# A decode block on one core: part of the wq load over eight engines, the last K tiles in between V tiles, and two products 512 columns wide with a fold

## The chip, the cores and the metric

The kernel runs on one core of a Trainium2 chip. The metric is the device time of one execution in microseconds. The kernel before takes 1319.78 us, the median of three runs (1319.77 to 1319.85).

## The reference

One token per sequence, batch 2, goes through a layer norm; then attention over a cache of 32768 positions with 8 KV heads (4 query heads each) and a gated MLP are computed from the same normed row, and their product is added to the input. All data are float32.

```python
xn = layernorm(x)                                        # [2, 1, 512]
q = (xn @ wq)                                            # 512 x 4096: 32 heads of 128
p = softmax(q @ k_cache.T * 128 ** -0.5)                 # caches: [2, 8, 32768, 128]
s = (p @ v_cache) @ wo                                   # wo: 4096 x 512
gate, up = xn @ W_gate, xn @ W_up                        # 512 x 1792 each
g = silu((gate * (gate > 0) * up) @ W_down)              # W_down: 1792 x 512
return x + s * g
```

## The kernel before

The caches are 64 tiles of 8.4 MB: each of the 16 pairs of batch and KV head (a "group", `g`) has two K tiles and two V tiles (`u` = 0, 1), and a tile holds 16384 positions as 128 partitions of 64 KB. With wq (8.4 MB), the two MLP input weights in one slot (`gu`), W_down (`wd`) and wo (8.4 MB) they all pass through one ring of three slots of 64 KB per partition (`slot`, `SLOTS`). A load is issued on SyncE's queue (`load`) and waits there until the tile three places earlier in the ring has been read for the last time. SyncE's queue is in order, so a load that waits holds back all loads behind it.

For a group, `scores(g)` lets VectorE turn each K tile in 32x32 blocks, in place, in eight parts of 128x2048 (`turn`), lets TensorE multiply the turned halves with the query (`score`, 16 matmuls a half) and lets VectorE take maxima (`peak`). `soft(g)` finds the maximum of the group, takes exponents on ScalarE, brings the weights into V's order with a matmul by a permutation (`perm`) and a transpose on VectorE, and sums them. `values(t)` is 32 matmuls of 512 columns on a V tile, into four column groups of the PSUM tile `o_ps`. `finish_group(g)` scales and masks the result into `os`; after every second group four matmuls with `place` add it to `ot_ps`. A float32 matmul stands twice in the profile: `x64` there is 32 matmuls of the source.

The loop over groups runs under a manual schedule: on each engine, instructions stand in the order in which the code is written. A group loads K, K, V, V. At the end wo comes in six pieces of 16, 8, 4, 2, 1 and 1 rows of 512 columns (a row is one `i`; partition p holds rows of its own), `ot` is taken out of `ot_ps`, and 32 rows times four column blocks of 128 are multiplied into `py` (128 small matmuls, `L418`). Two VectorE operations with `gy` (the MLP's result, computed at the start by `mlp_down`) and `xy` (the input) give the output, which leaves in four small DMAs.

The start: wq's load is the first, `gu` and `wd` follow into the other two slots, and the first K tile takes wq's slot when `project_q` has read it.

Of the kernel before, what the change touches and what calls it, by code (L numbers as in the profile page):

```python
# [20 lines left out]
SLOTS = 3  # L21
ALIGN = 512
WO_PIECES = (16, 8, 4, 2, 1, 1)


@with_exitstack
def kernel(
# [39 lines left out]
    def load(dst, src):  # L67
        nc.sync.dma_start(dst, src)

    wqs = slot("wq")  # L70
    load(wqs, wq.rearrange("(p i) n -> p (i n)", p=P))
    wqt = wqs.rearrange("p (i n) -> p i n", i=NKC)

    row = work.tile([P, 512], F32, tag="row", name="xp", bufs=3)
    xp = row[:32, :]
# [83 lines left out]
    xnp = const.tile([P, NKC, 32], F32, name="xnp")  # L159
# [3 lines left out]
    nc.vector.tensor_copy(xnp.rearrange("p k m -> p (k m)"), m_ps[:, : NKC * 32])  # L163

    def project_q():
        pick = ident.rearrange("p (c m) -> p c m", c=4)[:, :, :B]
        nq = 2 * REP * 4 * B
        spread = work.tile([P, 4, 4, Q], F32, tag="row", name="spread", bufs=3)
        for kb in range(4):
            nc.vector.tensor_copy(  # L170
                spread[:, :, kb, :], ident.rearrange("p (e l) -> p e l", e=4)
            )
        for half in range(2):
            pq = S[0][half]
            for i in range(NKC):
                for c in range(4):
                    n0 = (half * 4 + c) * 512
                    nc.tensor.matmul(  # L178
                        pq[32 * c : 32 * c + 32, :],
                        xnp[:, i, :],  # L180
                        wqt[:, i, n0 : n0 + 512],
                        start=(i == 0),
                        stop=(i == NKC - 1),
                    )
        for half in range(2):
            qs = work.tile([P, 512], F32, tag="row", name=f"qs_{half}", bufs=3)
            nc.vector.tensor_copy(qs, S[0][half])  # L187
# [56 lines left out]

    def mlp_down(ht):
        for i in range(FI):
            for c in range(4):
                nc.tensor.matmul(
                    m_ps[32 * c : 32 * c + 32, :P],
                    ht[:, i, :],  # L250
                    wdt[:, i, c * P : (c + 1) * P],
                    start=(i == 0),
                    stop=(i == FI - 1),
                )
        nc.scalar.activation(gy, m_ps[:, :P], AF.Silu)

    def group(g):
        return g % B, g // B

    def load_tile(src, t, name):  # L260
        b, hk = group(t // NU)
        lo = (t % NU) * TK
        dst = slot(name)
        load(dst, src[b, hk, lo : lo + TK, :].rearrange("(p r) d -> p (r d)", p=P))
        return dst

    MX, LS, W, RL, OS = {}, {}, {}, {}, {}

    def turn(t, s):
        k = KT[t]  # L270
        for c in range(NC):
            part = slice((s * NC + c) * NJ * DH, (s * NC + c + 1) * NJ * DH)
            nc.vector.transpose(k[:, part], k[:, part])  # L273

    def score(t, s):
        g, u = divmod(t, NU)
# [18 lines left out]
    def scores(g):  # L295
        halves = [(g * NU + u, s) for u in range(NU) for s in range(NS)]
        turn(*halves[0])
        for before, after in zip(halves, halves[1:] + [None]):
            if after:
                turn(*after)  # L300
            score(*before)
            peak(*before)

    def soft(g):
# [20 lines left out]
        for u in range(NU):  # L325
            for s in range(NS):
# [3 lines left out]
                    w, S[u][s], AF.Exp, bias=nb, scale=SCALE, accum_out=LS[g][:, i : i + 1]  # L330
                )
                nc.tensor.matmul(pt_ps, perm[:, s, :], w, start=(s == 0), stop=(s == NS - 1))  # L332
            pt = work.tile([P, NJ, Q], F32, tag="pt", name=f"pt_{g}_{u}")
            nc.vector.transpose(pt.rearrange("p j m -> p (j m)"), pt_ps)  # L334
            PT[g * NU + u] = pt
# [51 lines left out]
    mlp_down(ht)  # L387

    with tc.manual_schedule(engines=None):
        for g in range(NG):  # L390
            for u in range(NU):
                KT[g * NU + u] = load_tile(kc, g * NU + u, f"k_{g}_{u}")
            for u in range(NU):
                VT[g * NU + u] = load_tile(vc, g * NU + u, f"v_{g}_{u}")
            scores(g)
            soft(g)
            if g % 3 == 2 and g // 3 < 4:
                c = g // 3
                nc.scalar.dma_start(xy[32 * c : 32 * c + B, :], x[:, 0, c * P : (c + 1) * P])
            for u in range(NU):  # L400
                values(g * NU + u)
            finish_group(g)

        wos = slot("wo")
        worows = wo.rearrange("(p i) d -> p (i d)", p=P)
# [4 lines left out]
        for b in range(B):  # L410
            nc.vector.tensor_reduce(
                ot[:, :, b], ot_ps[:, b].rearrange("p c i -> p i c"), axis=AX.X, op=ALU.add
            )
        py = S[0][0]
        wot = wos.rearrange("p (i d) -> p i d", i=WI)
        for i in range(WI):
            for c in range(4):
                nc.tensor.matmul(  # L418
                    py[32 * c : 32 * c + B, :P],
                    ot[:, i, :],  # L420
                    wot[:, i, c * P : (c + 1) * P],
                    start=(i == 0),
                    stop=(i == WI - 1),
                )
        nc.vector.tensor_mul(res, py[:, :P], gy)
        nc.vector.tensor_add(res, res, xy)
        for c in range(4):
# [35 lines left out]
```

## Time and profile before

| | |
|---|---|
| median of three runs | 1319.78 us |
| the profiled execution's own time | 1318.75 us |
| its span, first to last instruction | 1316.9 us |
| TensorE busy | 838.3 us (64%) |
| VectorE busy | 674.7 us (51%) |
| ScalarE busy | 49.8 us (4%) |
| read from memory | 564.67 MB, 429 GB/s over the span |
| granted TensorE clock, mean | 0.854 |

An engine's busy share says little here, since the stages have different limits. What is to be looked at is the share of the sixteen DMA engines' time, and then the last 30 us, where loads run out and the output still has to be computed. In the profile, PE is TensorE (PEld its weight loads), DVE VectorE, ACT ScalarE, POOL GpSimd, SP SyncE. A row of a timeline is the start, the length, engine, line, operation and how many, and in brackets the idle time before it and what ended that. In a table of stretches, each engine's busy time stands with its number of instructions, then the granted clock of TensorE, the mean busy share of the DMA engines and GB/s.

### The profile page before, as it was taken

The numbers are of one execution on the slowest core, as the hardware profiler recorded it, in microseconds if no ns is written. First come the engines' busy times: TensorE is split into PE (matmuls) and PEld (weight loads), VectorE is DVE, ScalarE is ACT, GpSimd is POOL, SyncE is SP. The second block draws the span as 40 slices with busy tenths as digits, with TensorE's granted clock in tenths as the row PEclk, the third lists the DMA queues.
The fourth block names the chain that finished last, engine by engine and source line by source line (L and its number), as shares of the span: only waits on it lengthen the run. The fifth ranks groups of instructions, "written<-read, shape, count | busy, mean of one in ns | idle before, by whom it ended". The sixth has DMA issues, their size and how long they took to land.

```text
span 1316.9 us, 10829 instructions
## 1 busy us (share of the span) xinstructions
PE 838.3 (64%) x4892; PEld 214.5 (16%) x4892; DVE 674.7 (51%) x569; ACT 49.8 (4%) x133; POOL 0.7 (0%) x6
## 2 busy tenths in 40 slices
PE   3467466765756577575667756665675767667467
PEld 1212011110211112021121201111121111212013
DVE  3183562917447191744719265380936638183560
ACT  0000000000000000000000000000000000000000
POOL 0000000000000000000000000000000000000000
PEclk9779698988888789787888969798888878988789
DMA  9999999999999999999999999999999999999996
GB/s 407 436 442 421 442 438 426 432 438 433 430 430 440 437 424 439 434 428 442 423 435 444 423 436 442 426 432 438 427 438 428 436 435 428 444 424 433 444 422 290
DMA packets 10738, 565.36 MB, mean 429 GB/s; under 512 B 1202, under 2 KB 1218, under 8 KB 1604
## 3 DMA queue, kind: packets, MB, share of 16 engines
q1 hardware_dynamic: 10664, 564.66, 99.1%
q8 instruction: 38, 0.62, 0.2%
q14 instruction: 8, 0.07, 0.0%
q10 hardware_dynamic: 28, 0.01, 0.0%
HBM read 564.67 MB, written 0.00 MB: 429 GB/s over the span
## 4 chain that ended last, share of the span: by engine, by line
DMA 48%; DVE 27%; PE 23%; issue 2%; ACT 0%; SPq 0%; ACTq 0%; DVEq 0%
DMA k<-in_A_k_cache_dram 45%; DVE k L273 22%; PE o_ps L351 9%; PE pt_ps L332 7%; PE s L280 5%; DMA gu<-in_B_W_up_dram 3%; DVE mx L293 2%; DVE pt L334 2%; PE s L418 1%; DVE mrow L316 0%; PE m_ps L319 0%; PE m_ps L338 0%; PE m_ps L307 0%; ACT w L329 0%; DVE mr L309 0%
## 5 line engine op out<-in xcount | busy, mean ns | idle before, releaser
L280 PE MATMUL s<-k,qt 128*32 128x512 f32 x2048 | 465.0, 687 | 362.8 <-DVE k L273 362.6
L273 DVE STREAM_TRANSPOSE k<-k 128x2048 f32<-128x2048 f32 x256 | 566.8, 2276 | 193.0 <-DMA k<-in_A_k_cache_dram 187.3
L351 PE MATMUL o_ps<-v,pt 128*16 128x512 f32 x2048 | 223.4, 592 | 0.2
L280 PEld LDWEIGHTS s<-k,qt 128*32 128x32 f32 x2048 | 87.9, 121 | 735.8 <-DVE k L273 593.1
L363 DVE SCALAR_TENSOR_TENSOR os<-o_ps,rl,mask 128x512 f32<-128x512 f32 x16 | 12.0, 750 | 220.3 <-PE o_ps L351 220.3
L332 PE MATMUL pt_ps<-w,perm 128*128 128x512 f32 x128 | 86.0, 808 | 32.3 <-ACT w L329 17.9
L329 ACT ACTIVATE w<-s,nb 128x512 f32<-128x512 f32 x64 | 43.3, 685 | 1178.4 <-DVE nb L323 1176.4
L351 PEld LDWEIGHTS o_ps<-v,pt 128*16 128x16 f32 x2048 | 57.9, 97 | 151.3 <-issue 146.7
L334 DVE STREAM_TRANSPOSE pt<-pt_ps 128x512 f32<-128x512 f32 x32 | 22.9, 717 | 104.3 <-PE pt_ps L332 104.3
L293 DVE TENSOR_REDUCE mx<-s 128x1 f32<-128x512 f32 x64 | 42.3, 662 | 58.4 <-PE s L280 58.4
L332 PEld LDWEIGHTS pt_ps<-w,perm 128*128 128x128 f32 x128 | 27.1, 234 | 74.2 <-ACT w L329 37.3
L375 PE MATMUL ot_ps<-os,place 128*128 128x256 f32 x64 | 16.0, 392 | 7.0 <-DVE os L363 7.0
L338 PE MATMUL m_ps<-l,same 128*128 128x1 f32 x32 | 6.1, 260 | 13.5 <-DVE l L337 13.5
L307 PE MATMUL m_ps<-ident,m 128*1 128x128 f32 x16 | 4.3, 270 | 15.7 <-DVE m L306 15.7
L375 PEld LDWEIGHTS ot_ps<-os,place 128*128 128x128 f32 x64 | 11.5, 189 | 15.6 <-DVE os L363 14.4
L319 PE MATMUL m_ps<-negs,mrow 1*128 1x1 f32 x32 | 6.0, 256 | 11.7 <-DVE mrow L316 11.7
L178 PE MATMUL s<-wq,xnp 128*32 128x512 f32 x64 | 9.0, 725 | 6.5 <-DMA wq<-in_A_wq_dram 6.5
L329 ACT ACTIVATION_READ_ACCUMULATOR w<-s,nb 128x1 f32 x64 | 12.8, 200 | 0.0
L162 PE MATMUL m_ps<-ident,xc 32*128 32x32 f32 x4 | 0.7, 300 | 15.7 <-DVE xc L158 15.7
L338 PEld LDWEIGHTS m_ps<-l,same 128*128 128x128 f32 x32 | 4.8, 188 | 31.9 <-DVE l L337 31.9
L222 PE MATMUL s<-gu,xnp 128*32 128x448 f32 x64 | 7.4, 542 | 2.5 <-DMA gu<-in_B_W_up_dram 2.5
L187 DVE COPY qs<-s 128x512 f32<-128x512 f32 x2 | 1.4, 692 | 14.5 <-PE s L178 14.5
(62 smaller groups left out, 83.3 us busy)
## 6 DMA issues: line engine op xcount, KB each, us to landing
wo<-in_A_wo_dram SPq DMA_DIRECT2D x1, 4096.0 KB
gu<-in_B_W_gate_dram SPq DMA_DIRECT2D x1, 3584.0 KB
gu<-in_B_W_up_dram SPq DMA_DIRECT2D x1, 3584.0 KB
wd<-in_B_W_down_dram SPq DMA_DIRECT2D x1, 3584.0 KB, 47.5
wo<-in_A_wo_dram SPq DMA_DIRECT2D x1, 2048.0 KB
wo<-in_A_wo_dram SPq DMA_DIRECT2D x1, 1024.0 KB
k<-in_A_k_cache_dram SPq DMA_DIRECT2D x32, 36.8
v<-in_A_v_cache_dram SPq DMA_DIRECT2D x32, 38.1
```

Of the source, the lines that this page charges most:

```text
L178: nc.tensor.matmul(pq[32 * c : 32 * c + 32, :], xnp[:, i, :], wqt[:, i, n0 : n0 + 512], start=(i == 0), stop=(i == NKC - 1),)
L273: nc.vector.transpose(k[:, part], k[:, part])
L280: nc.tensor.matmul(S[u][s][Q * c : Q * c + Q, :], qt[:, g, e, :], mov[:, s, c, e], start=(e == 0), stop=(e == 3),)
L293: nc.vector.reduce_max(MX[g][:, i : i + 1], S[u][s], axis=AX.X)
L329: nc.scalar.activation(w, S[u][s], AF.Exp, bias=nb, scale=SCALE, accum_out=LS[g][:, i : i + 1])
L332: nc.tensor.matmul(pt_ps, perm[:, s, :], w, start=(s == 0), stop=(s == NS - 1))
L334: nc.vector.transpose(pt.rearrange("p j m -> p (j m)"), pt_ps)
L338: nc.tensor.matmul(m_ps[:, 300:301], same.rearrange("p r h -> p (r h)"), l, start=True, stop=True)
L351: nc.tensor.matmul(o_ps[Q * a : Q * a + NC * REP], w[:, j, s * NC * REP : (s + 1) * NC * REP], v[:, s, j], start=(u == 0 and s == 0 and j ...
L363: nc.vector.scalar_tensor_tensor(OS[hk][:, b], o_ps, RL.pop(g), mask.unsqueeze(2).to_broadcast([P, NC, DH]), op0=ALU.mult, op1=ALU.mult,)
L375: nc.tensor.matmul(ot_ps.rearrange("p b c i -> p (b c) i"), place[:, lo : lo + P], src[:, dq], start=(hk == 0 and dq == 0), stop=(hk == HK ...
L418: nc.tensor.matmul(py[32 * c : 32 * c + B, :P], ot[:, i, :], wot[:, i, c * P : (c + 1) * P], start=(i == 0), stop=(i == WI - 1),)
```

## The change

The diff has four parts.

1. wq's load becomes two: 13824 of the 16384 columns of each partition as before, and the other 2560 (10 KB per partition, the first 2560 columns of each partition's first row) with a pattern whose outermost size in memory is 8. The second takes memory rows in another order, so a fifth small transpose makes a copy of the normed row in that order (`xnp[:, 4]`), and `project_q` takes that for the matmuls whose columns come from this piece.
2. `mlp_down` multiplies rows of 512 columns into four column groups (14 matmuls where there were 56), copies the PSUM tile, and adds the four groups up by four matmuls with `fold`, a constant made from the identity.
3. The last two groups are written out. K tile 15_0 is loaded ahead of V tile 14_0, and K tile 15_1 between V tiles 14_0 and 14_1. Three of the eight parts of K 15_0 are turned inside `scores(14)` and `soft(14)`; the scores of group 15 come between the two `values` of group 14. The last V tile comes in two halves.
4. The output product does 28 of wo's rows as matmuls of 512 columns into four column groups of `pw` (cleared before), copies the result, multiplies rows 28 and 29 in the old form, folds, and multiplies rows 30 and 31 in the old form.

```diff
+SHIFT = 2560
+WO_WIDE = 28
...
-    load(wqs, wq.rearrange("(p i) n -> p (i n)", p=P))
+    load(wqs[:, : SLOT - SHIFT], wq.rearrange("(p i) n -> p (i n)", p=P)[:, SHIFT:])
+    load(
+        wqs[:, SLOT - SHIFT :],
+        wq.rearrange("(t a i) n -> i a t n", a=8, i=NKC)[0, :, :, :SHIFT],
+    )
...
+    fold = const.tile([P, Q], F32, name="fold")
+    nc.vector.tensor_reduce(
+        fold, ident.rearrange("p (a m) -> p m a", a=4), axis=AX.X, op=ALU.add
+    )
...
     def mlp_down(ht):
         for i in range(FI):
-            for c in range(4):
...
+            a = i % 4
+            nc.tensor.matmul(
+                m_ps[32 * a : 32 * a + 32, :],
+                ht[:, i, :],
+                wdt[:, i, :],
+                start=(i < 4),
+                stop=(i >= FI - 4),
+            )
+        part = work.tile([P, 512], F32, tag="row", name="down", bufs=3)
+        nc.vector.tensor_copy(part, m_ps)
+        for c in range(4):
+            nc.tensor.matmul(pt_ps[32 * c : 32 * c + 32, :P], fold, part[:, c * P : (c + 1) * P], ...)
+        nc.scalar.activation(gy, pt_ps[:, :P], AF.Silu)
...
+        for u in range(NU):
+            load_k(g, u)
+        for u in range(NU):
+            load_k(h, u)
+            load_v(g, u)
+        for u in range(NU):
+            load_v(h, u, NS if u == NU - 1 else 1)
+        first = [(h * NU, 0, c) for c in range(NC)]
+        scores(g, ahead=first[:1])
+        soft(g, ahead=first[1 : 1 + NU])
+        for u in range(NU):
+            if u == NU - 1:
+                scores(h, range(NU - 1))
+                scores(h, [NU - 1])
+            values(g * NU + u)
+        finish_group(g)
+        soft(h)
+        for u in range(NU):
+            values(h * NU + u)
+        finish_group(h)
...
+        nc.vector.memset(pw, 0.0)
+        for i in range(WO_WIDE):
+            a = i % 4
+            nc.tensor.matmul(pw[32 * a : 32 * a + B, :], ot[:, i, :], wot[:, i, :], ...)
+        part = work.tile([P, 512], F32, tag="row", name="wide", bufs=3)
+        nc.vector.tensor_copy(part, pw)
+        narrow(range(WO_WIDE, WI - 2))
+        for c in range(4):
+            nc.tensor.matmul(py[32 * c : 32 * c + B, :P], fold[:, :B], part[:, c * P : (c + 1) * P], ...)
+        narrow(range(WI - 2, WI))
```

SyncE's queue from group 14 on, before: two K tiles, two V tiles, the same for group 15, then wo.

```order
L68 DMA k_14_0_3032<-in_A_k_cache_dram 128x16384
L68 DMA k_14_1_3034<-in_A_k_cache_dram 128x16384
L68 DMA v_14_0_3036<-in_A_v_cache_dram 128x16384
L68 DMA v_14_1_3038<-in_A_v_cache_dram 128x16384
L68 DMA k_15_0_3225<-in_A_k_cache_dram 128x16384
L68 DMA k_15_1_3227<-in_A_k_cache_dram 128x16384
L68 DMA v_15_0_3229<-in_A_v_cache_dram 128x16384
L68 DMA v_15_1_3231<-in_A_v_cache_dram 128x16384
L68 DMA wo_3421<-in_A_wo_dram 128x8192
```

The same queue after the change.

```order
L70 DMA k_14_0_3001<-in_A_k_cache_dram 128x16384
L70 DMA k_14_1_3003<-in_A_k_cache_dram 128x16384
L70 DMA k_15_0_3005<-in_A_k_cache_dram 128x16384
L70 DMA v_14_0_3007<-in_A_v_cache_dram 128x16384
L70 DMA k_15_1_3009<-in_A_k_cache_dram 128x16384
L70 DMA v_14_1_3011<-in_A_v_cache_dram 128x16384
L70 DMA v_15_0_3013<-in_A_v_cache_dram 128x16384
L70 DMA v_15_1_3015<-in_A_v_cache_dram 128x8192 x2
L70 DMA wo_3391<-in_A_wo_dram 128x8192
```

Each load waits for the tile three places ahead of it: V 14_1 now waits for the scores of K 15_0, where it waited for those of K 14_1.

TensorE from `values(14, 0)` to the end, before (`s_0_0` is S[0][0], the four score tiles; `w` is one half's exponents).

```order
L351 MATMUL o_ps_121<-v_14_0_3036,pt_14_0_3144 16x512 x32
L351 MATMUL o_ps_121<-v_14_1_3038,pt_14_1_3152 16x512 x32
L280 MATMUL s_0_0_117<-k_15_0_3225,qt_112 32x512 x16
L280 MATMUL s_0_1_118<-k_15_0_3225,qt_112 32x512 x16
...
L351 MATMUL o_ps_121<-v_15_0_3229,pt_15_0_3337 16x512 x32
L351 MATMUL o_ps_121<-v_15_1_3231,pt_15_1_3345 16x512 x32
L375 MATMUL ot_ps_124<-os_7_3223,place_103 128x256 x4
L418 MATMUL s_0_0_117<-wo_3421,ot_114 2x128 x128
```

The same stretch after the change.

```order
L391 MATMUL o_ps_124<-v_14_0_3007,pt_14_0_3124 16x512 x32
L315 MATMUL s_0_0_120<-k_15_0_3005,qt_115 32x512 x16
L315 MATMUL s_0_1_121<-k_15_0_3005,qt_115 32x512 x16
L315 MATMUL s_1_0_122<-k_15_1_3009,qt_115 32x512 x16
L315 MATMUL s_1_1_123<-k_15_1_3009,qt_115 32x512 x16
L391 MATMUL o_ps_124<-v_14_1_3011,pt_14_1_3133 16x512 x32
...
L415 MATMUL ot_ps_127<-os_7_3286,place_104 128x256 x4
L502 MATMUL s_0_1_121<-wo_3391,ot_117 2x512 x28
L491 MATMUL s_0_0_120<-wo_3391,ot_117 2x128 x8
L513 MATMUL s_0_0_120<-wide_3429,fold_111 2x128 x4
L491 MATMUL s_0_0_120<-wo_3391,ot_117 2x128 x8
```

The scores of group 15 stand ahead of `values(14, 1)`, and 112 of the 128 small output matmuls have become 28 wide ones and four of the fold.

VectorE after the change, from the end of `scores(14)` into `scores(15)`; before, the eight parts of K 15_0 stood in one row behind `finish_group(14)`.

```order
L304 STREAM_TRANSPOSE k_15_0_3005<-k_15_0_3005 128x2048
L328 TENSOR_REDUCE mx_14_3042<-s_1_1_123 128x1
...
L361 COPY nb_14_3114<-m_ps_126 128x1
L304 STREAM_TRANSPOSE k_15_0_3005<-k_15_0_3005 128x2048
L374 STREAM_TRANSPOSE pt_14_0_3124<-pt_ps_125 128x512
L304 STREAM_TRANSPOSE k_15_0_3005<-k_15_0_3005 128x2048
L374 STREAM_TRANSPOSE pt_14_1_3133<-pt_ps_125 128x512
...
L304 STREAM_TRANSPOSE k_15_0_3005<-k_15_0_3005 128x2048 x5
```

One part of K 15_0 stands ahead of group 14's last maximum, two more in the gaps of `soft(14)`, and five behind it.

More of the change, by code (lines that the diff above doesn't have):

```diff
@@ L162 @@
         nc.tensor.transpose(m_ps[:, i * 32 : (i + 1) * 32], xcol[:, i, :], ident[:32, :32])
-    nc.vector.tensor_copy(xnp.rearrange("p k m -> p (k m)"), m_ps[:, : NKC * 32])
+    nc.tensor.transpose(m_ps[:, NKC * 32 : (NKC + 1) * 32], sq[:, :P], ident[:32, :32])
+    nc.vector.tensor_copy(xnp.rearrange("p k m -> p (k m)"), m_ps[:, : (NKC + 1) * 32])
     def project_q():
@@ L246, in mlp_down, with load_tile @@
         for i in range(FI):
-            for c in range(4):
[L248 to L255, printed above, removed]
+            a = i % 4
[5 more added lines that the diff above has]
+                stop=(i >= FI - 4),
+            )
+        part = work.tile([P, 512], F32, tag="row", name="down", bufs=3)
+        nc.vector.tensor_copy(part, m_ps)
+        for c in range(4):
+            nc.tensor.matmul(
+                pt_ps[32 * c : 32 * c + 32, :P],
+                fold,
+                part[:, c * P : (c + 1) * P],
+                start=True,
+                stop=True,
+            )
+        nc.scalar.activation(gy, pt_ps[:, :P], AF.Silu)
     def group(g):
         return g % B, g // B
-    def load_tile(src, t, name):
+    def load_tile(src, t, name, pieces=1):
         b, hk = group(t // NU)
@@ L263, in load_tile, with turn_part @@
         dst = slot(name)
-        load(dst, src[b, hk, lo : lo + TK, :].rearrange("(p r) d -> p (r d)", p=P))
+        rows = src[b, hk, lo : lo + TK, :].rearrange("(p r) d -> p (r d)", p=P)
+        n = SLOT // pieces
+        for i in range(pieces):
+            load(dst[:, i * n : (i + 1) * n], rows[:, i * n : (i + 1) * n])
         return dst
     MX, LS, W, RL, OS = {}, {}, {}, {}, {}
+    turned_parts = set()
+    def turn_part(t, s, c):
+        if (t, s, c) not in turned_parts:
+            turned_parts.add((t, s, c))
+            part = slice((s * NC + c) * NJ * DH, (s * NC + c + 1) * NJ * DH)
+            nc.vector.transpose(KT[t][:, part], KT[t][:, part])
     def turn(t, s):
-        k = KT[t]
         for c in range(NC):
-            part = slice((s * NC + c) * NJ * DH, (s * NC + c + 1) * NJ * DH)
-            nc.vector.transpose(k[:, part], k[:, part])
+            turn_part(t, s, c)
     def score(t, s):
@@ L293, in peak, with scores @@
         nc.vector.reduce_max(MX[g][:, i : i + 1], S[u][s], axis=AX.X)
-    def scores(g):
-        halves = [(g * NU + u, s) for u in range(NU) for s in range(NS)]
+    def scores(g, us=range(NU), ahead=()):
+        halves = [(g * NU + u, s) for u in us for s in range(NS)]
         turn(*halves[0])
@@ L300, in scores, with soft @@
                 turn(*after)
+            else:
+                for part in ahead:
+                    turn_part(*part)
             score(*before)
             peak(*before)
-    def soft(g):
+    def soft(g, ahead=()):
         m = work.tile([P, 1], F32, tag="m", name=f"m_{g}")
@@ L332, in soft @@
                 nc.tensor.matmul(pt_ps, perm[:, s, :], w, start=(s == 0), stop=(s == NS - 1))
+            for part in ahead[u : u + 1]:
+                turn_part(*part)
             pt = work.tile([P, NJ, Q], F32, tag="pt", name=f"pt_{g}_{u}")
@@ L389, with load_k, load_v, residual @@
     with tc.manual_schedule(engines=None):
[L390 to L396, printed above, removed]
+        def load_k(g, u):
+            KT[g * NU + u] = load_tile(kc, g * NU + u, f"k_{g}_{u}")
+        def load_v(g, u, pieces=1):
+            VT[g * NU + u] = load_tile(vc, g * NU + u, f"v_{g}_{u}", pieces)
+        def residual(g):
             if g % 3 == 2 and g // 3 < 4:
@@ L399 @@
                 nc.scalar.dma_start(xy[32 * c : 32 * c + B, :], x[:, 0, c * P : (c + 1) * P])
+        for g in range(NG - 2):
+            for u in range(NU):
+                load_k(g, u)
+            for u in range(NU):
+                load_v(g, u)
+            scores(g)
+            soft(g)
+            residual(g)
             for u in range(NU):
@@ L413, with narrow @@
             )
-        py = S[0][0]
+        py, pw = S[0]
         wot = wos.rearrange("p (i d) -> p i d", i=WI)
[L416 to L424, printed above, removed]
+        def narrow(rows):
+            for i in rows:
+                for c in range(4):
+                    nc.tensor.matmul(
+                        py[32 * c : 32 * c + B, :P],
+                        ot[:, i, :],
+                        wot[:, i, c * P : (c + 1) * P],
+                        start=(i == WO_WIDE),
+                        stop=(i == WI - 1),
+                    )
+        nc.vector.memset(pw, 0.0)
+        for i in range(WO_WIDE):
+            a = i % 4
+            nc.tensor.matmul(
+                pw[32 * a : 32 * a + B, :],
+                ot[:, i, :],
+                wot[:, i, :],
+                start=(i < 4),
+                stop=(i >= WO_WIDE - 4),
+            )
+        part = work.tile([P, 512], F32, tag="row", name="wide", bufs=3)
+        nc.vector.tensor_copy(part, pw)
+        narrow(range(WO_WIDE, WI - 2))
+        for c in range(4):
+            nc.tensor.matmul(
+                py[32 * c : 32 * c + B, :P],
+                fold[:, :B],
+                part[:, c * P : (c + 1) * P],
+                start=False,
+                stop=False,
+            )
+        narrow(range(WI - 2, WI))
         nc.vector.tensor_mul(res, py[:, :P], gy)
```

17 lines of the change are left out of this document (13 added, 4 removed).

## The prediction

> **What bounds the kernel now.** I read the page's DMA parts first, then stretches of the last 30 us, then the timeline there. From the page:
>
> ```profile
> span 1316.9 us, 10829 instructions
> ...
> q1 hardware_dynamic: 10664, 564.66, 99.1%
> q8 instruction: 38, 0.62, 0.2%
> ...
> HBM read 564.67 MB, written 0.00 MB: 429 GB/s over the span
> ...
> k<-in_A_k_cache_dram SPq DMA_DIRECT2D x32, 36.8
> v<-in_A_v_cache_dram SPq DMA_DIRECT2D x32, 38.1
> ```
>
> The loads keep sixteen DMA engines busy for 99.1% of the span; the other 0.9% is 12 us for each engine on average, and no edit that leaves the bytes alone can win more than that. A tile of 8.39 MB at 429 GB/s takes 19.6 us, and a tile lands 37 to 38 us after its issue: the next load stands in the queue some 18 us before it is needed. Compute in the middle costs nothing. What is left is the end, where I asked for the busy time by stretches (DMA's share is the last but one column):
>
> ```profile
> 1290.00:1303.00 13.00, 12.13 (x109) 3.68 (x101) 0.75 (x1) 0.00 (x0) 0.00 (x0) 1.00 0.97 414
> 1304.20:1307.80 3.60, 3.19 (x120) 3.07 (x124) 0.35 (x2) 0.00 (x0) 0.00 (x0) 1.00 0.54 227
> 1308.10:1309.20 1.10, 1.10 (x49) 1.03 (x37) 0.00 (x0) 0.00 (x0) 0.00 (x0) 1.00 0.47 179
> 1309.50:1310.40 0.90, 0.00 (x0) 0.00 (x0) 0.00 (x0) 0.00 (x0) 0.00 (x0) 1.00 0.29 100
> ```
>
> The engines don't end together. With 0.97 for sixteen, 0.54 is nine engines, 0.47 eight, 0.29 five: seven are done by 1304.2, an eighth near 1308, the others between 1309.2 and 1311. The page has a cause for it: queue 8, instructions, took 0.2% of 16 x 1316.9 us, 42 us (32 to 53 by rounding); if eight engines carry it, that is 5.3 us for each (4 to 6.6), about the gap between 1304 and 1309-1311. Then the timeline of the end:
>
> ```profile
> 1275.08 2.70 SPq L68 DMA_DIRECT2D wo<-in_A_wo_dram  x6
> ...
> 1301.23 0.75 DVE L363 SCALAR_TENSOR_TENSOR os<-o_ps,rl,mask 128x512 f32<-128x512 f32 x1 [13.72 <-PE o_ps L351]
> 1302.04 1.99 PE L375 MATMUL ot_ps<-os,place 128*128 128x256 f32 x8 [0.87 <-DVE os L363]
> 1304.07 0.49 DVE L411 TENSOR_REDUCE ot<-ot_ps 128x32 f32<-128x128 f32 x2 [2.08 <-PE ot_ps L375]
> 1304.61 4.86 PE L418 MATMUL s<-wo,ot 128*2 128x128 f32 x169 [0.58 <-DVE ot L411]
> 1310.82 2.58 PE L418 MATMUL s<-wo,ot 128*2 128x128 f32 x87 [1.35 <-issue]
> 1313.46 0.29 DVE L425 TENSOR_TENSOR res<-s,gy 128x128 f32<-128x128 f32 x1 [8.90 <-PE s L418]
> 1314.10 0.63 SPq L429 DMA_DIRECT2D out_dram<-res  x2
> ```
>
> ```profile
> wo<-in_A_wo_dram SPq DMA_DIRECT2D x2, 256.0 KB, 33.6
> ```
>
> The six loads of wo are issued from 1275.08 on, the last at about 1277.3; 33.6 us later, at 1310.9, wo is whole (L, below). TensorE stands still for 1.35 us with nothing to wait for, and ends at 1313.40, 2.5 us behind L, since 87 of its 256 passes were still to do. From 1313.46 to the span's end are 3.44 us that no edit touches.
>
> **The change part by part.**
>
> *wq in two loads.* The page gives one engine 429/16 = 26.8 GB/s. If eight engines carry the second piece, each takes 16 x 10 KB where it took 8 x 10 KB, and the others none: 81,920 bytes, 3.06 us more for eight, 3.06 us less for eight. If the eight are the early ones, the late half ends at 1306.2 to 1307.9, the seven early ones near 1307, and the early half's last, near 1308 now, at 1311.0. L moves by about nothing: from 1310.9 to 1311.0. That is the point where I choose: no row names an engine. Packet by packet (which no view prints) I saw the two-row transfers of x always on engines of the early half, which fits engines counted from the first; I take the early eight. The bounds are -3.06 us (nothing late among the eight) and +3.06 us (the eight are the late ones). [...]
>
> The start has room. wq is needed at 22.83, and its slot is refilled at 31.88:
>
> ```profile
> 22.83 8.99 PE L178 MATMUL s<-wq,xnp 128*32 128x512 f32 x64 [6.47 <-DMA wq<-in_A_wq_dram]
> 31.88 12.92 SPq L68 DMA_DIRECT2D k<-in_A_k_cache_dram  x2
> 49.75 5.34 PE L248 MATMUL m_ps<-wd,ht 128*32 128x128 f32 x112 [5.34 <-DMA wd<-in_B_W_down_dram]
> ```
>
> 3 us later, K 0_0 is issued at 35, still 14 us before the load ahead of it (`wd`) lands at 49.7. The extra copy, transpose and `fold` reduction (0.4 us at most each, like L121's reduction of the identity) fall before 22.8, where everything waits for wq. Cost 0; without that cover up to 3 us.
>
> *The down product.* 112 passes in 5.34 us become 28 of 110 ns (below), a copy of 0.69 and 8 small passes: 4.1 us instead of 5.3, beside loads. 0, or 1 us if the queue had no lead.
>
> Single operations by line and shape (the last number ahead of the second bar is the mean in ns):
>
> ```profile
> L273 DVE STREAM_TRANSPOSE k<-k 128x2048 f32<-128x2048 f32 x256 | 566.8, 2276 | 193.0 <-DMA k<-in_A_k_cache_dram 187.3 <-issue 5.6
> L418 PE MATMUL s<-wo,ot 128*2 128x128 f32 x256 | 7.4, 273 | 1.9 <-issue 1.4 <-DVE ot L411 0.6
> L187 DVE COPY qs<-s 128x512 f32<-128x512 f32 x2 | 1.4, 692 | 14.5 <-PE s L178 14.5
> L121 DVE TENSOR_REDUCE place<-ident 128x4 f32<-128x128 f32 x1 | 0.4, 366 | 0.0
> L145 DVE MEMSET o_ps<- 128x512 f32 x1 | 0.5, 485 | 0.1
> ```
>
> *The order of the last loads.* Times of a pass (64 in 7.04 us are 110 ns each), and of the last tiles:
>
> ```profile
> 106.64 3.63 PE s L280 x26
> ...
> 1174.27 8.89 DVE k L273 x4
> ...
> 1206.62 0.72 DVE pt L334
> ...
> 1207.81 7.04 PE o_ps L351 x64
> ...
> 1253.11 8.89 DVE k L273 x4
> ```
>
> K 14_1 landed at 1174.2, K 15_1 four tiles later at 1253.1: 19.7 us a tile on the slowest engine. After the change K 15_0 lands near 1194, V 14_0 near 1213.7, K 15_1 at 1233.4, V 14_1 at 1253.1. V 14_1 takes K 15_0's slot, so it is issued when TensorE has done `values(14, 0)` and both halves of `score(15, 0)`; behind it in the queue stand V 15_0, V 15_1 and wo. VectorE is ready: `soft(14)` ended at 1207.3, with the two parts in its gaps perhaps at 1209.5, and five parts of 2.28 us end near 1221. TensorE starts at 1213.7 with 64 passes (7.04 us) and then 64 more of the same width: 1227.8 at the full clock. The clock may be half there:
>
> ```profile
> 1224.90:1233.70 8.80, 0.00 (x0) 0.00 (x0) 0.00 (x0) 0.00 (x0) 0.00 (x0) 0.50 1.01 439
> 1233.80:1241.80 8.00, 5.16 (x6) 0.54 (x6) 8.00 (x4) 0.00 (x0) 0.00 (x0) 0.50 1.00 434
> ```
>
> Here the idle TensorE fell to 0.50 and stayed there for 8 us of new work. With 8 us at half rate 36 passes are done by 1221.7, and the other 92 (110 ns) by 1231.8. The slowest engine needs V 14_1 at 1233.4, so it doesn't wait; engines 3 to 4 us ahead of it stand idle for that lead, which they don't need. Cost 0, bounds 0 and 2.5 us (TensorE at 1235, plus a start of 1 us).
>
> *What the order wins.* Group 15's scores and `soft` are done by about 1273. The last V tile lands one wo load (19.6 us) before L, at 1291.4, and only its second half is left: 32 passes, 3.5 us, or 7.0 at half clock. From `os`'s start to the first output pass took 1301.23 to 1304.61, 3.4 us; with the clearing of `pw` (0.49, as L145's) 3.9, cold 6. So TensorE has `ot` at 1298.8 to 1304.4, where it had it at 1304.6.
>
> *The output product.* 28 wide rows are 56 passes of 110 ns, 6.2 us. wo's pieces land in proportion to L: 16 rows at 1301.2, 24 at 1306.1, 28 at 1308.5, 30 at 1309.8, 31 at 1310.4. So the wide part ends at 1308.5 + 0.9 = 1309.4, the copy (0.69, as L187's) at 1310.1, rows 28 and 29 and the fold at 1310.5; behind L = 1311.0 come row 31's 8 passes at 29 ns (4.86 us / 169) and one pass's length, 273 ns: 1311.5 instead of 1313.4. The 1.35 us of standing still go too, as 448 quick instructions become 112 slower ones.
>
> Sum: -1.9 us (bounds 0, if TensorE is at half clock and ends the wide rows at 1311.5 or later, and -1.9); wq +0.1; the rest 0: -1.8 to -1.9. The profiled execution took 1318.75, 1.0 below the median; on the median 1319.78 - 1.9 = 1317.9. I take 0.2%, 2.6 us, as what a measurement of this kernel can tell from no change; 1317.9 is inside.
>
> **The rivals.**
>
> *Faster: L moves by the whole 3 us.* It needs that none of the eight that take more is late: the engine that ends near 1308 would have to be among the eight relieved, or its lateness be gone. Against it: 0.54 ahead of 1308 is nine engines, so the early half has only seven. For it: nine and eight differ by 0.07 in a share of few packets. L = 1307.9, the wide rows end at 1306.3 to 1309.5: -5.0, 1314.8.
>
> *Slower through the relieved engines being the early ones.* L = 1314.0, and the tail's 1.9 are won: +1.2, 1321.0. This is still within 0.2%.
>
> *Slower for good: V 14_1 is issued too late.* TensorE, cold through all 128 passes, needs 28.2 us from 1213.7: 1241.9, 8.5 past the need; all engines stand idle and everything behind moves: 8.5 - 1.9 = +6.6, 1326.4. It decides where TensorE ends later than 1237.9 (1233.4 + 1.9 + 2.6). For it: the half clock above. Against it: 8 us of work ended it there.
>
> *The change does not do what it says:* the 10 KB go over all sixteen anyway. Then L stays at 1310.9: 1317.8, as in the forecast.
>
> **How the numbers follow.** Forecast 0.52, the same time by sixteen engines 0.06, faster through L 0.22, the wrong eight 0.12, V 14_1 late 0.08. Its own range is 1317.2 to 1319.8 (tail between -1.9 with L some tenths lower and 0). For 8 in 10 I add the faster rival and leave out the two slower ones but for the nearer part of the first: 1314.6 to 1320.3. Faster by over 0.2% (below 1317.1): 0.22 and 0.04 of the forecast's low side, 0.26. Slower by over 0.2% (above 1322.4): 0.08 and 0.01, 0.09. Same: 0.65.
>
> **What would show it.** L: the last wo load's time to landing, and a DMA share in the last 4 us of one engine (0.06), not five to nine; if the share falls from 0.97 to nothing within 1.5 us, the faster rival is right. The order: `L391` on V 14_0 near 1213.7, V 14_1's issue by 1232, and no fall of the DMA share near 1234; a share under 0.8 there for more than the early engines' 4 us is the slow rival. The tail: the wide passes (`L502`) start by 1301.5 in three bursts that wait for wo, and TensorE ends 0.5 us behind L. The forecast is wrong if L falls below 1310.2, or if the wide passes run at 220 ns in the last burst.

## The result and the profile after

The changed kernel takes 1328.9 us (median of 6 runs, 1328.57 to 1330.51), the kernel before 1319.8 beside it on the same chip: 1.0076 of its time, with an interval of 1.0063 to 1.0089. It is 9 us slower, where the forecast was 1.9 us faster and its range ended at 1320.3. The profiled execution took 1328.65 us.

The page of the changed kernel:

```profile
span 1326.8 us, 10365 instructions
...
GB/s 289 423 426 441 429 441 424 439 433 431 433 429 441 429 437 429 443 427 433 433 437 427 437 437 427 435 433 439 427 435 433 435 431 433 435 435 435 422 426 310
...
q1 hardware_dynamic: 10944, 564.67, 99.2%
q8 instruction: 36, 0.59, 0.2%
...
HBM read 564.67 MB, written 0.00 MB: 426 GB/s over the span
```

The bytes are the same and the loads still fill 99% of sixteen engines' time. By the share of busy time nothing has happened. The rate row tells it: the first of the forty slices moved 289 GB/s where the others, the last aside, move 422 to 443.

So I asked for stretches of the start, first of the kernel before, then of the changed one (DMA share and GB/s are the last two columns):

```profile
18.00:37.00 19.00, 14.17 (x106) 5.98 (x110) 2.91 (x8) 1.28 (x1) 0.00 (x0) 1.00 0.96 414
...
21.00:34.00 13.00, 11.17 (x81) 4.47 (x82) 1.61 (x3) 0.00 (x0) 0.00 (x0) 1.00 0.98 421
37.00:53.00 16.00, 8.21 (x114) 4.59 (x110) 4.44 (x9) 0.00 (x0) 0.00 (x0) 0.82 1.06 455
```

```profile
18.00:37.00 19.00, 0.37 (x4) 0.23 (x8) 0.00 (x0) 0.00 (x0) 0.00 (x0) 1.00 0.99 181
...
21.00:34.00 13.00, 0.00 (x0) 0.00 (x0) 0.00 (x0) 0.00 (x0) 0.00 (x0) 1.00 1.06 166
37.00:53.00 16.00, 15.26 (x120) 6.08 (x112) 4.55 (x13) 1.28 (x1) 0.00 (x0) 1.00 1.00 431
```

While the 10 KB pieces run, the engines count as busier than before (1.06 against 0.98) and move 166 GB/s instead of 421. From 18 to 37 us, 19 x (414 - 181) / 429 = 10.3 us of loading are lost. How many transfers of the loads' queue stood in those 13 us, before and after:

```profile
q1 hardware_dynamic: 223, 5.48, 97.7%
```

```profile
q1 hardware_dynamic: 139, 2.16, 106.0%
```

139 transfers took 106% of 16 x 13 us, 1.59 us each on average, where 223 took 0.91. Packet by packet (which no view prints) a 10 KB piece takes 0.385 us at first and mostly 0.8 to 1.17 us from 19.3 on, and the packets of 28 KB of the gate weights beside them take mostly 2.8 to 3.2 us instead of 1.06: the engines that do not carry the piece are slowed as well. The 128 pieces took 130.1 us in all between 18.8 and 35.7 us, 7.7 at a time: eight engines. Which eight, and which partitions each of them writes, no row shows; in what follows an engine's partitions are read off the pattern of the load, as an assumption.

The timeline of the start of the changed kernel shows who waits:

```profile
36.63 8.71 PE L194 MATMUL s<-wq,xnp 128*32 128x512 f32 x64 [20.84 <-DMA wq<-in_A_wq_dram]
...
45.40 11.47 SPq L70 DMA_DIRECT2D k<-in_A_k_cache_dram  x2
...
61.81 6.32 PE L264 MATMUL m_ps<-wd,ht 128*32 128x512 f32 x28 [5.33 <-DMA wd<-in_B_W_down_dram]
```

wq is whole at 36.63 (22.83 before), K 0_0 is issued at 45.40 (31.88) and W_down is there at 61.81 (49.75). The queue never ran dry: 37 to 53 has 431 GB/s again. What is lost is the rate of those 19 us, and the loss reaches the end undiminished. The end, by the changed kernel's timeline:

```profile
1284.15 0.33 SPq L70 DMA_DIRECT2D wo<-in_A_wo_dram  x1
...
1308.60 0.75 DVE L403 SCALAR_TENSOR_TENSOR os<-o_ps,rl,mask 128x512 f32<-128x512 f32 x1 [25.19 <-PE o_ps L391]
...
1313.30 3.61 PE L502 MATMUL s<-wo,ot 128*2 128x512 f32 x32 [1.91 <-DMA wo<-in_A_wo_dram]
1318.08 1.90 PE L502 MATMUL s<-wo,ot 128*2 128x512 f32 x16 [1.17 <-DMA wo<-in_A_wo_dram]
1320.53 1.04 PE L502 MATMUL s<-wo,ot 128*2 128x512 f32 x8 [0.55 <-DMA wo<-in_A_wo_dram]
1321.64 0.69 DVE L510 COPY wide<-s 128x512 f32<-128x512 f32 x1 [9.12 <-PE s L502]
...
1322.60 0.85 PE L491 MATMUL s<-wo,ot 128*2 128x128 f32 x16
1323.52 0.29 DVE L521 TENSOR_TENSOR res<-s,gy 128x128 f32<-128x128 f32 x1 [1.19 <-PE s L491]
```

```profile
wo<-in_A_wo_dram SPq DMA_DIRECT2D x2, 256.0 KB, 38.9
```

1284.15 + 38.9 = 1323.0 is L, the moment at which wo is whole: 12 us later than before. From there to the result's start it is 0.5 us, where it was 2.5. The tail does what was forecast; wq does not.

### The profile page after: what moved, and what is told of

The parts are those of the page before. It is cut to its first block, busy times and chain, and to the rows that moved or that the text cites. A ratio compares the mean times of both kernels' runs of the same rounds, so it can differ in the third digit from the quotient of the medians.

```text
span 1326.8 us, 10365 instructions
## 1 busy us (share of the span) xinstructions
PE 839.5 (63%) x4657; PEld 206.5 (16%) x4657; DVE 677.2 (51%) x574; ACT 49.5 (4%) x133; POOL 0.7 (0%) x6
## 4 chain that ended last, share of the span: by engine, by line
DMA 52%; DVE 24%; PE 22%; issue 2%; ACT 0%; another core or an unknown queue 0%; ACTq 0%; SPq 0%; DVEq 0%
DMA k<-in_A_k_cache_dram 41%; DVE k L304 19%; PE o_ps L391 8%; DMA v<-in_A_v_cache_dram 6%; PE pt_ps L370 6%; PE s L315 5%; DMA wo<-in_A_wo_dram 3%; DMA wq<-in_A_wq_dram 3%; DVE mx L328 2%; DVE pt L374 2%; PE s L194 1%; PE s L238 1%; DVE mrow L354 0%; PE m_ps L378 0%; PE m_ps L357 0%
## 5 line engine op out<-in xcount | busy, mean ns | idle before, releaser
L315 PE MATMUL s<-k,qt 128*32 128x512 f32 x2048 | 460.0, 693 | 342.0 <-DVE k L304 341.9
L391 PE MATMUL o_ps<-v,pt 128*16 128x512 f32 x2048 | 229.9, 604 | 15.0 <-DMA v<-in_A_v_cache_dram 14.9
L378 PE MATMUL m_ps<-l,same 128*128 128x1 f32 x32 | 6.3, 267 | 13.5 <-DVE l L377 13.5
L264 PE MATMUL m_ps<-wd,ht 128*32 128x512 f32 x28 | 6.3, 1006 | 5.3 <-DMA wd<-in_B_W_down_dram 5.3
```

The source lines that it names most:

```text
L315: nc.tensor.matmul(S[u][s][Q * c : Q * c + Q, :], qt[:, g, e, :], mov[:, s, c, e], start=(e == 0), stop=(e == 3),)
L378: nc.tensor.matmul(m_ps[:, 300:301], same.rearrange("p r h -> p (r h)"), l, start=True, stop=True)
L391: nc.tensor.matmul(o_ps[Q * a : Q * a + NC * REP], w[:, j, s * NC * REP : (s + 1) * NC * REP], v[:, s, j], start=(u == 0 and s == 0 and j ...
```

## Experiments

### The piece, and the rest without it

The first four kernels ran beside 21 runs of the kernel before (median 1319.28). The changed kernel with wq in one load:

```diff
-    load(wqs[:, : SLOT - SHIFT], wq.rearrange("(p i) n -> p (i n)", p=P)[:, SHIFT:])
-    load(wqs[:, SLOT - SHIFT :], wq.rearrange("(t a i) n -> i a t n", a=8, i=NKC)[0, :, :, :SHIFT])
+    load(wqs, wq.rearrange("(p i) n -> p (i n)", p=P))
```

> The changed kernel with wq in one load again; the wide products and the new order of the last loads stay. Theory M (the 10 KB piece alone costs the time: between 19 and 36 us all sixteen engines ran at 166 GB/s instead of 421): the slow stretch goes, the last landing is again near 1311, and what is left is the tail's gain forecast at 1.9 us: 1317.9. Rival N (the new order of the last loads costs it, the late issue of V 14_1): still above 1325.

Measured: 1316.67 us, 0.9983 of before (0.9975 to 0.9992). The kernel before with only the piece:

```diff
-    load(wqs, wq.rearrange("(p i) n -> p (i n)", p=P))
+    load(wqs[:, : SLOT - SHIFT], ...)
+    load(wqs[:, SLOT - SHIFT :], wq.rearrange("(t a i) n -> i a t n", a=8, i=NKC)[0, :, :, :SHIFT])
```

> The kernel before with only wq's load in two. Theory M: 11 to 12 us later than before, 1331, as the tail's 1.9 us are not won here. Rival N: 1319 to 1323.

Measured: 1331.42 us, 1.0094 (1.0078 to 1.0109). The piece alone costs 12 us, and without it the rest of the change gains 2.6. Its stretch from 21 to 34 us is that of the changed kernel:

```profile
21.00:34.00 13.00, 0.00 (x0) 0.00 (x0) 0.00 (x0) 0.00 (x0) 0.00 (x0) 1.00 1.06 164
```

### Where the piece is read from

The rows that the piece reads lie 64 KB apart. Here it reads one stretch of 1.3 MB instead:

```diff
-        wq.rearrange("(t a i) n -> i a t n", a=8, i=NKC)[0, :, :, :SHIFT],
+        wq[: P * SHIFT // QN].rearrange("r n -> (r n)").rearrange("(t a n) -> a t n", a=8, n=SHIFT),
```

> The changed kernel; the 10 KB pieces come from 1.3 MB of wq in one piece, 10 KB from engine to engine, instead of from rows 64 KB apart. They are not the right elements, so q is not the reference's. Eight engines and the partitions they write stay. Theory A (memory side: eight engines read rows 64 KB apart in step): pieces take 0.39 us each, the stretch at 166 GB/s goes, 1318. Theory B (partition side: eight engines write blocks of 16 partitions in step): no change, 1328.9, pieces of 1.1 us. Theory C (an eight-engine copy of such pieces is slow whatever it reads and writes): also 1328.9.

Measured: 1329.57 us, 1.0079 (1.0065 to 1.0092), and again 1.06 of share at 164 GB/s from 21 to 34 us. How the reads lie in memory is not it. What was left were the partitions that are written (theory B), and the use of only eight engines (theory C).

### Where the piece is written to

The next four ran beside 22 runs of before (median 1318.54). Two kernels load 1.23 MB more than the kernel before, on eight engines, and differ in the partitions alone: in the first the eight engines of a load write partitions 4 apart, in the second eight neighbours.

```diff
+    flat = wq[: 5 * 24 * PIECE // wq.shape[1]].rearrange("r n -> (r n)")
+    flat = flat.rearrange("(j t a n) -> j a t n", j=5, t=3, a=8, n=PIECE)
+    for j in range(5):
+        part = slice(32 * (j // 4) + j % 4, 32 * (j // 4) + j % 4 + 29, 4)   # second kernel: slice(8 * j, 8 * j + 8)
+        load(wds[part, FI * D : FI * D + 3 * PIECE].rearrange("p (t n) -> p t n", t=3), flat[j])
```

> The kernel before with five extra loads right behind wq's, 24 pieces of 10 KB each (1.23 MB in all, 15 pieces on each of eight engines), from one stretch of memory into partitions 4 apart (0, 4, .. 28 in one load), so that no two engines write into neighbouring partitions. The bytes are read into an unused part of a slot. Theory B (where the eight engines write is what is slow: in the change they write blocks of 16 neighbouring partitions, all in step): the pieces take about 0.39 us as the undisturbed ones of the change, the stretch keeps about 400 GB/s per busy engine, and the time is +0 to +6 us (15 x 0.385 = 5.8 us more on eight engines), 1319 to 1325. Theory C (a copy on eight engines beside full loads on the others is slow wherever it writes): pieces of 1.1 us, all engines slow for some 16 us, over 1331.

> The same five extra loads, but each into 8 neighbouring partitions (0 to 7, 8 to 15, ..), one partition for each of eight engines. Theory B: all eight write into one small block at a time, so it is as slow as the change or slower: pieces of 1.1 us or more and a time over 1330. Theory C: pieces of 1.1 us as well, over 1331, no different from the loads 4 partitions apart. If both are fast, neither theory holds and it is the form of the load (16 partitions to an engine) that matters.

Measured: 1322.03 us (1.0026, 1.0015 to 1.0037) with partitions 4 apart, 1335.77 us (1.0134, 1.0119 to 1.0149) with neighbours. One line of the code, 13.7 us. Their stretches, 4 apart first:

```profile
21.00:34.00 13.00, 10.91 (x81) 4.43 (x81) 1.61 (x3) 0.05 (x1) 0.00 (x0) 1.00 0.99 423
```

```profile
21.00:34.00 13.00, 9.66 (x69) 3.12 (x69) 1.08 (x2) 0.00 (x0) 0.00 (x0) 1.00 1.03 130
```

Packet by packet, all 120 pieces took 0.385 us in the first; in the second they took 1.0 to 1.54 us after the first few, at most four times that. So a copy on eight engines is not slow as such, and theory C falls.

Two more kernels are the changed one with the piece over sixteen engines: in the first each writes a block of 8 neighbouring partitions, all in step; in the second the piece is loaded like any other.

```diff
-        wq.rearrange("(t a i) n -> i a t n", a=8, i=NKC)[0, :, :, :SHIFT],
+        wq[: P * SHIFT // QN].rearrange("r n -> (r n)").rearrange("(t a n) -> a t n", a=16, n=SHIFT),   # blocks of 8
+        wq.rearrange("(p i) n -> p (i n)", p=P)[:, :SHIFT],                                           # ordinary
```

> The changed kernel with the 10 KB piece over sixteen engines, each writing a block of 8 neighbouring partitions one after another, all in step, from one stretch of memory (q is then not the reference's). Theory B: the piece is slow still, at least in part: a stretch of full DMA share with well under 400 GB/s, and a time between 1319 and 1329. Theory C: sixteen engines are as good as any ordinary load: 1316.7 as with wq in one load.

> The changed kernel with the 10 KB piece as an ordinary second load of 128 rows: engines and partitions as in every other load. Theories B and C alike: no slow stretch, 1316.7 as with wq in one load. If two loads or pieces of 10 KB as such are what is slow, over 1320.

Measured: 1319.85 us (1.0015, 1.0005 to 1.0024) with blocks, 1316.72 us (0.9987, 0.9978 to 0.9997) as an ordinary load, against 1316.67 with wq in one load. Two loads cost nothing; blocks in step cost 3.1 us, with pieces of 0.64 to 0.82 us after the first twenty, half of all at 0.77 or more, twice 0.385.

### A piece that should not collide, and is slow still

Theory B said that the step of 16 partitions was the fault. So the same bytes went over eight engines with 4 partitions between them, and 6 KB over four engines with 8 between them (`STEP_A` is 8 or 4):

```diff
+    wq_rows = wq.rearrange("(h r a i) n -> h i a r n", h=4, a=STEP_A, i=NKC)
+    for h in range(4):
+        load(wqs[32 * h : 32 * h + 32, SLOT - SHIFT :], wq_rows[h, 0, :, :, :SHIFT])
```

> The changed kernel with the same 10 KB piece over the same number of engines (eight), but in four loads of 32 partitions in which engine a writes partitions 4a to 4a+3: the engines in step are 4 partitions apart instead of 16, and one row of the input is taken in the order that fits. Theory B (the step of 16 partitions is what is slow): no stretch of full share and low GB/s, the 10.9 us are back, and only the bytes count. In the changed kernel's last 5 us three engines' worth of share was left (0.17 to 0.20), so L = 1323.0 - 10.9 = 1312.1, 1.1 later than with one load: 1317.8, or 1319.7 if a late engine carries the full 3.06 us. Theory C (eight engines are slow wherever they write): 1328.9.

> The same with a piece of 6 KB per partition on four engines, which write 8 partitions apart. Each of the four takes 24 x 6 KB = 147,456 bytes more, 5.5 us, the other twelve 49,152 bytes less, 1.83 us. If the four are all among the engines that end near 1304, L falls from 1311.0 to 1309.2 or 1309.5: 1315.0 to 1315.3, the first version in which taking bytes off the late engines pays. If one of them is a late engine (1308 to 1311 before), L is 1313.5 to 1316.6: 1319 to 1322. If theory B is wrong about the step, a slow stretch comes back: over 1322.

Measured, beside a median of before of 1317.58: 1322.43 us (1.003, 1.0018 to 1.0042) and 1324.9 us (1.0054, 1.0042 to 1.0066). Both miss: 1317.8 and 1315 had been expected. The eight-engine version got back 6.5 of the changed kernel's 12.2 us beyond one load; the four-engine version, made to be faster than one load, took 8.2 us more than it. The profiled execution of the eight-engine version took 1334.56 us, 12 more than its other six: up to about 140 us its 64 KB packets took 2.71 us instead of 2.42, for a reason that isn't shown. So of that profile only the pieces, which come before 28 us, are read. By the order of the loads, the 64 pieces into partitions 0 to 63 took 0.385 us but for a dozen; the 64 into partitions 64 to 127 took 0.57 to 0.82 us, nearly all of them 0.75 or more. The half of the partitions is what differs, so one more kernel is the one with extra loads 4 apart, 64 partitions higher:

```diff
-        part = slice(32 * (j // 4) + j % 4, 32 * (j // 4) + j % 4 + 29, 4)
+        part = slice(64 + 32 * (j // 4) + j % 4, 64 + 32 * (j // 4) + j % 4 + 29, 4)
```

> The five extra loads of 24 pieces as in the run with partitions 4 apart, but 64 partitions higher: the same bytes, engines and distances, and one number changed. [...] Theory B in its sharper form (what counts is how many engines write into the same four partitions' worth of the array at once; two halve each other): pieces of about 0.8 us instead of 0.385, a stretch of full share at some 210 to 320 GB/s, and 15 x 0.4 = 6 us more on all engines: 1327 to 1328 where the lower half took 1322.0. Rival (only neighbours within one load count): pieces of 0.385 and 1322.

Measured: 1325.94 us (1.0065, 1.0048 to 1.0081), 3.9 us more than in the lower half, a little under what theory B expected; the rival's 1322 is out. Its stretch, and the transfers from 23 to 28 us in the lower half and in the upper half:

```profile
21.00:34.00 13.00, 10.63 (x77) 3.92 (x77) 1.38 (x2) 0.00 (x0) 0.00 (x0) 1.00 0.97 231
```

```profile
q1 hardware_dynamic: 178, 2.33, 109.0%
```

```profile
q1 hardware_dynamic: 93, 1.16, 107.2%
```

The same busy time, half the transfers. Nearly all pieces took 0.75 to 0.79 us, twice 0.385. So the distance within one load is not all that counts. My reading, an estimate from the times of the pieces: engines that write close together at the same moment take turns, whichever load they serve. A piece took 0.385 us with 4 apart in the lower half, and as an ordinary second load; 0.75 to 0.79, twice that, in the upper half; 0.77 or more for half of all in blocks of 8 over sixteen; up to 1.54, four times that, with neighbours; and up to 1.17, three times that, in the change, whose engines write 16 apart and where 93 of the 128 pieces took 0.9 or more. In the four-engine version the 6 KB pieces took 0.234 us at first and then 0.35 to 0.50, between one and about two times that. How many partitions make one place where engines take turns, and which engines meet there in the upper half and in the change, no run shows.

### The tail: the order and the wide product

The kernel before with only the new order of the last loads, and the last V tile in halves:

```diff
         for u in range(NU):
             load_k(g, u)
+        for u in range(NU):
+            load_k(h, u)
+            load_v(g, u)
         for u in range(NU):
-            load_v(g, u)
...
+            load_v(h, u, NS if u == NU - 1 else 1)
```

> The kernel before with only the new order of the last loads and the last V tile in halves. The output product is still 256 small passes behind ot. By the forecast's steps ot is ready at 1299 to 1304 instead of 1304.6, so TensorE's small passes (29 ns) catch up with wo and wait for its last row near 1311: the order gives 1 to 1.9 us of the tail's 1.9, 1318 to 1319. If the standing still of 1.35 us (instructions late) comes after wo's last row too, 1319 to 1319.8. Rival N: above 1325.

Measured: 1316.85 us, 0.9984 (0.9975 to 0.9993), as much as order, products and fold together (1316.67). The kernel before with only the wide output product:

```diff
+        nc.vector.memset(pw, 0.0)
+        for i in range(WO_WIDE):
+            ...
+        narrow(range(WO_WIDE, WI - 2))
+        # fold of pw
+        narrow(range(WI - 2, WI))
```

> The kernel before with the output product of 512 columns and its fold alone; loads in the old order. TensorE has ot at 1304.6 as before: the clearing to 1305.2, 56 passes of 110 ns to 1311.4, the copy to 1312.1, fold and the last 16 passes to 1313.0, where the old form ended at 1313.4: -0.4 us, 1318.9 beside a before of 1319.3, no change that can be measured. Rival, the wide rows are what takes the 1.35 us of standing still away and win by themselves: -1.9, 1317.4.

Measured: 1317.18 us beside 1317.58, 1.001 (0.9991 to 1.0029; this ratio goes by means, and one execution of the wide product took 1331.12): no difference that this shows. The kernel before varies by itself, from 1316.6 to 1320.0, while the kernels with the new order lie between 1316.47 and 1317.04. So two more profiles of it were taken:

> The kernel before, unchanged, for a second profile. Its executions spread from 1316.6 to 1320.0, while the kernels with the new order of the last loads lie within 0.5 us of 1316.7. Theory T1: TensorE's standing still at the end (1.35 us in the first profile, no releaser) comes and goes with the time of the last instruction fetch; an execution near 1317 shows none of it and TensorE's end under 1.5 us behind L, one near 1319 shows it. Theory T2: L itself moves by 2 us from run to run, and the tail behind it is the same.

> The same kernel once more, for a third profile, with the same two theories: T1, the distance from the last piece of wo to TensorE's end changes (2.3 us in the first profile) and L stays within 0.3 us of 1311; T2, L moves and the distance stays.

They took 1317.28 and 1317.92 us. The end of each, in this order:

```profile
1303.29 4.86 PE L418 MATMUL s<-wo,ot 128*2 128x128 f32 x169 [0.58 <-DVE ot L411]
1309.35 2.58 PE L418 MATMUL s<-wo,ot 128*2 128x128 f32 x87 [1.21 <-issue]
1311.98 0.29 DVE L425 TENSOR_TENSOR res<-s,gy 128x128 f32<-128x128 f32 x1 [8.75 <-PE s L418]
```

```profile
1303.81 4.86 PE L418 MATMUL s<-wo,ot 128*2 128x128 f32 x169 [0.58 <-DVE ot L411]
1309.99 2.58 PE L418 MATMUL s<-wo,ot 128*2 128x128 f32 x87 [1.33 <-issue]
1312.63 0.29 DVE L425 TENSOR_TENSOR res<-s,gy 128x128 f32<-128x128 f32 x1 [8.88 <-PE s L418]
```

Neither theory is right. The standing still is in all three profiles (1.21, 1.33, 1.35 us), each time after 169 passes, so it doesn't come and go. The last landing hardly moves (1310.9, 1311.4, 1311.1, from the completion events). What moves is the start of the output passes (1303.29, 1303.81, 1304.61), and the end follows it by 8.7 to 8.85 us: the end of the kernel before hangs on when TensorE gets to these passes, and on the pause in them, not on wo.

The start moves for two reasons. In the second of these profiles everything from group 15's scores on is 0.5 us later than in the first. In the third, the one shown ahead of the prediction, the last four `perm` passes ran at half the granted clock. Their stretch there, and then in the first of the three:

```profile
1282.30:1286.10 3.80, 3.75 (x4) 1.16 (x4) 0.00 (x0) 0.00 (x0) 0.00 (x0) 0.50 0.76 328
```

```profile
1282.80:1284.80 2.00, 1.95 (x4) 0.64 (x4) 0.01 (x1) 0.00 (x0) 0.00 (x0) 1.00 0.80 344
```

From group 15's first `perm` matmul to its first V matmul it took 8.7 us there, 7.6 in the other two: 1.1 us later.

T1's cause for the pause fits the packets all the same. In the three profiles a 16 KB instruction packet (queue 8) lands at 1307.99, 1308.62 and 1309.42, and the passes go on 1.36, 1.37 and 1.40 us later. In the runs with the piece alone and with the upper half, whose ends have the same 256 passes, such a packet lands some 2 us ahead of the 169th pass, and the passes go on without this pause. That TensorE waits for these instructions is argued from the times; no run changes them alone.

In the kernel with the new order alone `ot` is ready earlier, and the small passes wait for wo in bursts:

```profile
1301.48 3.68 PE L463 MATMUL s<-wo,ot 128*2 128x128 f32 x128 [0.58 <-DVE ot L456]
1306.20 2.25 PE L463 MATMUL s<-wo,ot 128*2 128x128 f32 x64 [1.04 <-DMA wo<-in_A_wo_dram]
1308.60 1.05 PE L463 MATMUL s<-wo,ot 128*2 128x128 f32 x32 [0.15 <-DMA wo<-in_A_wo_dram]
1309.83 1.03 PE L463 MATMUL s<-wo,ot 128*2 128x128 f32 x24 [0.18 <-DMA wo<-in_A_wo_dram]
1311.09 0.40 PE L463 MATMUL s<-wo,ot 128*2 128x128 f32 x8 [0.23 <-DMA wo<-in_A_wo_dram]
1311.56 0.29 DVE L470 TENSOR_TENSOR res<-s,gy 128x128 f32<-128x128 f32 x1 [10.14 <-PE s L463]
```

Now wo's last row sets the end, and that is the same every time. The small form keeps up with wo (0.09 us behind the wide form: 1311.56 against 1311.47 with wq in one load), so beside this order the wide product has nothing left to win. In the profile of the wide product alone, the passes start late and run through:

```profile
1302.95 0.49 DVE L415 TENSOR_REDUCE ot<-ot_ps 128x32 f32<-128x128 f32 x2 [2.09 <-PE ot_ps L379]
...
1304.08 6.19 PE L435 MATMUL s<-wo,ot 128*2 128x512 f32 x56 [1.17 <-DVE s L432]
1310.09 0.62 PE L424 MATMUL s<-wo,ot 128*2 128x128 f32 x16
1310.34 0.69 DVE L443 COPY wide<-s 128x512 f32<-128x512 f32 x1 [6.31 <-PE s L435]
...
1311.99 0.29 DVE L454 TENSOR_TENSOR res<-s,gy 128x128 f32<-128x128 f32 x1 [0.96 <-PE s L424]
```

From `ot`'s end (1303.44) to the result it is 8.55 us, against 8.75 to 8.9 in the three profiles of before: at the old order the wide form wins 0.2 to 0.35 us, close to the 0.4 expected.

## Why the prediction was wrong

- *wq in two loads, +0.1 with bounds of ±3.06.* This is the step that failed: the term was 12.0 us by the spans (1326.8 against 1314.8 with one load), and 12.1 alone on the kernel before by the medians (1331.42 against 1319.28). I priced the piece at an engine's usual rate, 26.8 GB/s, and bounded it only by which engines carry the bytes. The first pieces of the changed kernel do run at that rate (10,240 bytes in 0.385 us); then they take mostly 0.8 to 1.17, the packets of 28 KB beside them 2.8 to 3.2 us instead of 1.06, and the experiments above tie this to the partitions that are written (neighbours against 4 apart: 13.7 us). 10.3 us of the 12 are lost in the slow stretch. The bounds were wrong because no row of the profile of before has a load of this shape: every load of weights or cache there has 128 rows, and I took their rate for a property of an engine, whatever partitions it writes.
- *The eight that take more are the early ones.* Not borne out in full. The share at the end of the changed kernel shows some three engines alone for the last microseconds:

```profile
1318.00:1319.50 1.50, 1.42 (x16) 0.32 (x16) 0.00 (x0) 0.00 (x0) 0.00 (x0) 1.00 0.20 85
1319.50:1320.50 1.00, 0.48 (x8) 0.00 (x0) 0.00 (x0) 0.00 (x0) 0.00 (x0) 1.00 0.18 74
1320.50:1322.00 1.50, 1.26 (x17) 0.32 (x21) 0.36 (x1) 0.00 (x0) 0.00 (x0) 1.00 0.17 67
```

  Packet by packet, the sixteen engines end 11.2 us later on average than with wq in one load, and the last of them 12.0 us later. So some 0.8 us of L's move are these three engines': the mechanism of the "wrong eight" rival, at about a quarter of its price. Alone it would have left the time within 0.2%. The 0.9 us between 10.3 and 11.2 aren't told apart. That the piece goes over the early eight, on which the +0.1 rests, no run shows; what the runs showed is eight pieces at a time (above) and 12 us lost.
- *The start has room.* Right: wq was needed 13.8 us later, K 0_0 issued 13.5 us later, and the engines had work throughout. But room in the queue doesn't help where the engines' rate itself falls.
- *The down product, 0.* Right in cost, wrong in size. Its 28 passes were put at 110 ns and took 6.32 us in the changed kernel, 226 ns each (the granted clock was 0.50 from 61.8 to 66.9), so it got longer, not shorter. Beside loads that cost nothing: the run with one load has it, and its time is that of the order alone, which hasn't (1316.67, 1316.85).
- *The order, 0, and V 14_1 in time.* Right. In the changed kernel V 14_1 is issued at 1235.82, 8 us after the forecast's earliest, with every landing some 12 us later too; K 15_1 arrives at 1245.52 and the rival's 6 us of standing engines don't appear:

```profile
1226.23 9.52 PE L391 MATMUL o_ps<-v,pt 128*16 128x512 f32 x64 [4.50 <-DMA v<-in_A_v_cache_dram]
1235.57 7.04 PE L315 MATMUL s<-k,qt 128*32 128x512 f32 x64
1235.82 7.19 SPq L70 DMA_DIRECT2D v<-in_A_v_cache_dram  x2
...
1245.52 6.70 DVE L304 STREAM_TRANSPOSE k<-k 128x2048 f32<-128x2048 f32 x3 [2.13 <-DMA k<-in_A_k_cache_dram]
```

- *The tail, -1.9.* Right in size and in form (three bursts of wide passes, the end 0.5 us behind L): -2.1 by the spans of the profiles (1316.9 to 1314.8), -2.6 by the medians. Two things in its working were off. The whole of it comes from the order; the wide rows add next to nothing. And it is a gain on an execution like the profiled one: the fastest executions of the kernel before (1316.57) take no longer than those with the new order.
- *The faster rival* needed L at 1307.9; no kernel here had the last load before 1310.9. That a different choice of engines would get it isn't shown.

The best versions are the change without the piece (1316.67) and the order alone (1316.85), 0.2% faster than before.

## What to carry to other kernels

Before giving a load another shape, ask which partitions it will write at the same moment (neighbours took 13.7 us more here than 4 apart), and whether the same load is as cheap elsewhere (64 partitions higher it took 3.9 us more). The price was up to four times the 0.385 us of a piece, and the loads beside paid as well (28 KB packets took 2.8 to 3.2 us instead of 1.06). Moving bytes from one engine to another moves nothing off the partitions they go to: the three versions tried here took 12.2, 5.8 and 8.2 us beyond one load. A DMA share near 1 says that engines are occupied, not that they move: here 1.06 stood beside 166 GB/s, 0.98 beside 421. Read the GB/s of the same stretch beside it.

## What the hardware showed that I had not expected

- A piece of 10,240 bytes took 0.385 us, 26.6 GB/s, where nothing held it up, and near whole multiples of that elsewhere: 0.75 to 0.79 in the upper half, up to 1.17 in the change, up to 1.54 with neighbours. A place in the array that takes 26.6 GB/s, whether one engine writes there or four, would give these times; that is my estimate, and no run shows the place.
- The slowdown reaches the loads beside it. In the run with neighbours, the pieces go into partitions 0 to 39, and the gate weights' packets beside them took up to 4.0 us instead of 1.06. Eight engines at 10,240 bytes in 1.54 us would be 53 GB/s, and eight undisturbed ones 8 x 27 = 216; the whole moved 130. What the two loads share isn't shown.
- TensorE stood still for 1.2 to 1.35 us in the middle of ready work: after 169 small passes in all three profiles of the kernel before, until 1.36 to 1.40 us behind the landing of an instruction packet, and not in the two runs where that packet landed 2 us ahead.
